# Sparse attention and MoE on one core: V of two tiles loaded block by block, two weight blocks asked for by SyncE

## The chip, the core and the metric

One core of one Trainium2 chip. A time is the device time of one execution in microseconds; before the change it is 736.47 us, the median of 3 runs (736.07 to 736.59).

## What is computed

Block-sparse attention over 4 batches, 8 heads, 768 positions and 64 columns per head, and then a two-layer network on its output. Positions come in 24 blocks of 32. A query block sees its neighbours, the first and the last block, and three sampled blocks; the queries of the first and the last block see everything.

```python
mask = np.abs(blk_i - blk_j) <= window
mask = mask | (blk_i == 0) | (blk_j == 0) | (blk_i == n_blocks - 1) | (blk_j == n_blocks - 1)
for qb in range(n_blocks):
    for kb in sampled_blocks[qb]:
        mask[qb * block:(qb + 1) * block, kb * block:(kb + 1) * block] = True
...
attn = attn / (np.sum(attn, axis=-1, keepdims=True) + 1e-09)
return np.matmul(attn, v).astype(np.float32)
...
h = np.maximum(x @ w_in, 0.0)
return (h * h @ w_out).astype(np.float32)
```

Here x has 3072 rows of 512, w_in is 512 x 2048 and w_out 2048 x 512. The weights come as 64-bit floats.

## The kernel before

The 3072 rows are 24 tiles of 128 (4 query blocks each; batch b, tile t), and three tiles make a batch of the network, eight in all. `Half` is the attention of four heads of one tile, `Whole` that of two heads for the first and the last query block. A `Half` runs on PE scores (L478), on DVE the maxima (L490), on ACT the exponentials (L537), on PE the transposes (L552), on ACT and DVE the copies pT (L562, L564), on PE the product with V (L573), and on DVE the normalising (L587 to L590) and the transposing into x (L418). x is split into a high and a low part (xh L912, xl L916). The network's first layer is L928 (ph, from wi), its second L972 in the first batch (po, from WO and gp) and L982 in the later ones.

V of a tile is two tiles of four query blocks. The first (rows 0 to 63) holds the fixed rows, which are the first and the last key block and the same for all four query blocks, and below them two sampled blocks for each query block. The second holds the window and the third sampled block. For the first three tiles V lies in buffers of its own. `load_static` (L215) brings the fixed rows and `load_sampled` (L400) the sampled blocks, 65 KB each, through registers that SP loads with the indices. Both are issued by SP, which issues its DMAs in the order of the program and uses eight semaphores in turn: the ninth issue waits until the first has landed.

The weights come in blocks of 128 x 512, block f of w_in (part 0) and of w_out (part 1), in the order of the list `cuts`: three of part 0, then parts 1 and 0 in turn. A block goes through four stages, each of them called by `advance`:

- load: `cut_load` (L825), 512 KB of raw 64-bit words into a tile `craw` of a ring of seven buffers that the split weights share. POOL issues it.
- cut: two passes on ACT (L841, L843). The first ends at `W` for part 0 and at `WO` for part 1, or at `ct` for the very first block.
- bits: two passes on DVE (L852, L853).
- split: for blocks that are split, a cast on ACT (L890) and a difference on POOL (L893); for the first block L859 and L860 on POOL.

In the first batch the order of all engines is written out by hand. A counter `now` steps through the attention of the first three tiles; at the steps in `LOADS_0`, `CUTS_0`, `BITS_0` and `SPLIT_0` a stage advances. Three more loads are called in `prepare` and `rest` (L1076, L1091), which run at steps 8 and 35 and otherwise gather keys of the next tiles on POOL (L304, L322). Afterwards, in the network's first batch, `cut_next` cuts one block more and brings the other stages up to their distance from it: the load stage stands `AHEAD` = 4 blocks ahead. Each engine works its own instructions in order, so a load stands on POOL behind the key copies that were written before it, and a cut whose block has not landed holds up ACT.

Of the kernel before, what the change touches and what calls it, by code (L numbers as in the profile page):

```python
# [12 lines left out]
I32 = mybir.dt.int32  # L13
# [5 lines left out]
SP = mybir.EngineType.SP  # L19
# [4 lines left out]
BLK = 32  # L24
NBLK = S // BLK
NRAND = 3
P = 128
NT = S // P
NJ = P // BLK
# [13 lines left out]
HW = H * VW  # L43

NVB = NBLK + 2
V_STATIC = NBLK

UC = 3
# [25 lines left out]
LAG_2 = ({**LAG_0, "c": 3}, {**LAG_0, "t": 2})  # L74
SPLIT_0 = (54, 60)

LOADS_0 = (45, 50, 53, 56, 58)
CUTS_0 = (36, 46, 56, 58)
BITS_0 = (44, 50, 59, 60)
WI_0 = 47  # L80
# [26 lines left out]
def tile_block_sparse_attention_moe(ctx: ExitStack, tc, kd, knd, qd, qgd, vd, vnd, samp, const, wcat, out):  # L107
# [9 lines left out]
    nc = tc.nc  # L117
# [52 lines left out]
    VJ = {0: [one.tile([P, NJ, HW], F32, name=f"V{c}") for c in range(2)]}  # L170
# [5 lines left out]
    order = [(b, t) for b in range(B) for t in range(NT)]  # L176
# [14 lines left out]
    def values_of(k):  # L191

        return V[k if k < UC else 0]
# [4 lines left out]
    def halves(k, u):  # L198

        if k < UC:  # L200
            return slice(0, 2) if u == k // 2 else None
        return slice(u, u + 1)

    def columns(src, us):

        return src.rearrange("... (u c) -> ... u c", u=2)[..., us, :]

    def load_static(k, u, eng=nc.sync):
        us = halves(k, u)
        if us is None:  # L210
            return
        n = 1 if k == 0 else NJ
        if k < UC:
            src = vd[order[k][0], V_STATIC * BLK :].unsqueeze(1).broadcast_to([2 * BLK, n, HW])
            eng.dma_start(VJ[k][0][0 : 2 * BLK, 0:n], src)  # L215
            return
        for i in range(us.start, us.stop):
            src = columns(vd[order[k][0], V_STATIC * BLK :], i)
            src = src.unsqueeze(1).broadcast_to([2 * BLK, n, HW // 2])
            eng.dma_start(values_of(k)[0][0 : 2 * BLK, i, 0:n], src)  # L220

    def copy_static(i, copy):

# [4 lines left out]
    def place(k, j, n):  # L228

        return (j + n - 1 if 0 < k < UC else 1 + n) % NJ  # L230

    def windows(k, i):

        b, t = order[k]
        V1, vn = V[k][1][:, i], st["vn", b, i]

        def wide(copy):
            copy(V1, vn[:, t : t + 1].broadcast_to(list(V1.shape)))

        def narrow(copy, j, blk):  # L240
            at = slice(blk % NJ * BLK, (blk % NJ + 1) * BLK)
            copy(V1[at, j], vn[at, blk // NJ])

        return [
            wide,
            lambda copy: narrow(copy, 0, NJ * t - 1),
            lambda copy: narrow(copy, NJ - 1, NJ * t + NJ),
        ]
# [7 lines left out]
    def groups(t):  # L256

        return tuple(range(1 if t == 0 else 0, NJ - 1 if t == NT - 1 else NJ))
# [4 lines left out]
    def sampled(t, i, on):  # L263
        n = NJ * NRAND
        a = (2 * t + i) * n
        return nc.values_load_multi_w_load_instructions(
            st["idx"][0:1, a : a + n],
            engines=[on],
            min_val=0,
            max_val=NBLK - 2,  # L270
            skip_runtime_bounds_check_because="products of a block's index with 0 or 1, that is zero unless the index is 1 to 22",
        )[1]

    def load_q(b, t, eng=nc.sync, own=None):
        q = (own or rot).tile([P, NJ, NPAIR, BLK], F32, tag="q", name=f"q{b}_{t}", bufs=1 if own else 2)
        n = NJ * NPAIR * BLK
        eng.dma_start(q.rearrange("p a b c -> p (a b c)"), qd[b, :, t * n : (t + 1) * n])
        st["q", b, t] = q
# [31 lines left out]
    def key_windows(k, u, copy):  # L310

        b, t = order[k]
        kg, kn = st["kg", b, t][:, :, :, 2 * u : 2 * u + 2], st["kn", b, u]
        if 0 < k < UC:
            dst = kg[:, :, NJ:NK].rearrange("p j a i c -> p j a (i c)")
            src = kn[:, NJ * t : NJ * t + NJ].rearrange("p a i c -> p a (i c)").unsqueeze(1)
            copy(dst, src.broadcast_to(list(dst.shape)))
            return
        js = groups(t)
        c = NJ * t + js[0] - 1  # L320
        for n in range(3):
            copy(kg[:, js[0] : js[-1] + 1, NJ + place(k, 0, n)], kn[:, c + n : c + n + len(js)])  # L322
# [36 lines left out]
    def load_window(k, u, eng=nc.sync):  # L359
        us = halves(k, u)  # L360
        if us is None:
            return
        b, t = order[k]
        VB = values_of(k)[1]
        js = sorted(groups(t))
        j, c, n = js[0], NJ * t + js[0], len(js)
        if k < UC:
            src = vd[b, (c - 1) * BLK : (c + 1 + n) * BLK]
            src = bass.AP(src.tensor, src.offset, [[HW, 3 * BLK], [BLK * HW, n], [1, HW]])
            eng.dma_start(VJ[k][1][BLK:P, j : j + n], src)  # L370
            return
        for i in range(us.start, us.stop):
            src = vd[b, (c - 1) * BLK : (c + 1 + n) * BLK, i * HW // 2 : (i + 1) * HW // 2]
            src = bass.AP(src.tensor, src.offset, [[HW, 3 * BLK], [BLK * HW, n], [1, HW // 2]])
            eng.dma_start(VB[BLK:P, i, j : j + n], src)

    drawn = {}

    def load_sampled(k, u, eng, on, which=range(NRAND)):
        us = halves(k, u)  # L380
        if us is None:
            return
        b, t = order[k]
        VA, VB = values_of(k)
        if (b, t) not in drawn:
            drawn.clear()
            drawn[b, t] = sampled(t, 1, on)
        vals = drawn[b, t]
        if k < UC:
            v4 = vd[b].rearrange("(a p) c -> p a c", p=BLK)  # L390
        else:
            v4 = columns(vd[b], us).rearrange("(a p) u c -> p a u c", p=BLK)
        for j in sorted(groups(t)):
            for r in which:
                a = (place(k, j, 3) if r == 2 else 2 + r) * BLK
                if k < UC:
                    dst = VJ[k][r == 2][a : a + BLK, j]
                else:
                    dst = (VB if r == 2 else VA)[a : a + BLK, us, j]
                eng.dma_start(dst.unsqueeze(1), v4[:, bass.ds(vals[NRAND * j + r], 1)])  # L400

    def load_values(k, u, static=False):

        if static:
            load_static(k, u)
        load_window(k, u)
        load_sampled(k, u, nc.sync, SP)

    def x_tile(b, t):
        if (b, t) not in X:  # L410
            X[b, t] = rot.tile([P, NCC, P], F32, tag="x", name=f"x{b}_{t}", bufs=5)
        return X[b, t]
# [397 lines left out]
    cv = {}  # L810
# [11 lines left out]
    def cut_load(f, part):  # L822
        if wide:
            cv[f, part] = rot.tile([P, DM, 2], I32, tag="w", name=f"craw{f}_{part}", bufs=WBUFS)
            nc.gpsimd.dma_start(cv[f, part].rearrange("p a b -> p (a b)"), wcat[f, part].bitcast(I32))  # L825

    def cut(f, part):

# [39 lines left out]
    done = dict.fromkeys(stages, 0)  # L868

    def advance(stage):  # L870

        if done[stage] < len(cuts):
            stages[stage](*cuts[done[stage]])
        done[stage] += 1

    def cut_next():

        n = done["cut"] + 1
        for stage, to in (("cut", n), ("bits", n - 1), ("split", n - 2), ("load", n + AHEAD)):
            while done[stage] < to:  # L880
                advance(stage)

    def need(f, part):
# [3 lines left out]
    def split(c, src, name):  # L887
        w = rot.tile([P, 2, DM], F32R, tag="w", name=name, bufs=WBUFS)
        if c == 0:
            nc.scalar.copy(w[:, 0], src)  # L890
        else:
            nc.vector.tensor_copy(w[:, 0], src)  # L892
        nc.gpsimd.tensor_tensor(w[:, 1], src, w[:, 0], op=ALU.subtract)  # L893
        return w
# [165 lines left out]
    load_sampled(0, 0, nc.sync, SP)  # L1060
    load_window(0, 0)
    load_q(0, 1)
    load_q(0, 2, own=begin)
    load_static(1, 0)
    load_sampled(1, 0, nc.sync, SP, (0, 1))
    for k in range(UC):
        keys_of(0, k, begin if k == 2 else None)
    for k in range(1, UC):
# [7 lines left out]
    def prepare():  # L1076
        key_windows(1, 1, nc.gpsimd.tensor_copy)
        deque(keys[1], 0)
        for f in windows(1, 0) + windows(1, 1):
            f(nc.gpsimd.tensor_copy)  # L1080
        advance("load")
        load_static(2, 1)
        load_sampled(1, 0, nc.sync, SP, (2,))
        load_sampled(2, 1, nc.sync, SP, (0, 1))
        for _ in groups(2):
            next(keys[2])
        for f in windows(2, 1):
            f(nc.gpsimd.tensor_copy)
        advance("load")

    def rest():  # L1091
        key_windows(2, 1, nc.gpsimd.tensor_copy)
        deque(keys[2], 0)
        advance("load")

    fixed = [lambda i=i: copy_static(i, nc.scalar.copy) for i in range(2)]
    fixed += [lambda f=f: f(nc.scalar.copy) for f in windows(2, 0)]
# [7 lines left out]
    while work.todo or work.running or now < SPLIT_0[-1]:  # L1105
# [16 lines left out]
        if now in SPLIT_0:  # L1122
            f = 1 + SPLIT_0.index(now)
            wi1[0, f] = split(0, W1[f], f"wi0_{f}")
        for at, stage in ((CUTS_0, "cut"), (BITS_0, "bits"), (LOADS_0, "load")):
            if now in at:
# [85 lines left out]
```

## Time and profile before

| What | Value |
|---|---|
| median of 3 runs | 736.47 us |
| the profiled execution | 737.9 us |
| its span, first to last instruction | 735.4 us |
| mean granted clock of PE | 0.998 |
| PE busy in 20:30, 30:40, 40:50, 50:60, 60:70 | 9.53, 7.24, 6.87, 9.22, 8.18 of 10 us |
| DMA share in the same stretches | 1.01, 0.93, 0.67, 0.67, 0.82 |
| PE busy in 80:90 and in the five stretches of 10 us behind it | 10.00 of 10 us each |

In a row of a timeline the columns are start in us, duration in us, engine, line, operation, what is written from what is read, the count of merged instructions, and in brackets the idle time before with what ended it; "issue" there means that no semaphore in the profile ended it. In a row of windows they are the stretch, its length, the busy time of PE, PEld, DVE, ACT and POOL with counts, the granted clock, the share of the 16 DMA engines and GB/s. A row of a queue is packets, MB, share of 16 engines. A row of the DMA issues ends with the count, the KB of each and the median time from issue to landing. SPq is SP issuing a DMA; craw is a raw weight block.

### The profile page before, as it was taken

What the parts mean: (1) busy time and instruction counts of PE and PEld (TensorE: products, weight loads), DVE (VectorE), ACT (ScalarE), POOL (GpSimd) and SP (SyncE); (2) the same over time, 40 slices, a digit from 0 to 9 for tenths busy, and PEclk for the clock granted to TensorE, in tenths of its full rate; (3) what the DMA queues carried; (4) which work ended last, traced back from release to release, by engine and by line L of the source; (5) the groups of instructions that cost most, each with busy time, mean ns of one, the idle gap of its engine ahead of it and who ended that gap; (6) DMA issues with size and microseconds to landing.
All of it is one profiled execution on the core that took longest, in us unless ns stands there. A gap on an engine that the chain in (4) does not pass through costs nothing.

```text
span 735.4 us, 21490 instructions
## 1 busy us (share of the span) xinstructions
PE 706.9 (96%) x7496; PEld 566.9 (77%) x7496; DVE 531.3 (72%) x1057; ACT 500.4 (68%) x1117; POOL 554.8 (75%) x711
## 2 busy tenths in 40 slices
PE   5887999999999999999999999999999999999998
PEld 3564766678788888877878888887778888888986
DVE  5687888777686868678776877768878686647552
ACT  5777878988866866688876776578777776623222
POOL 8969969358776768869777587777876576868985
PEclk9999999999999999999999999999999999999999
DMA  9977798555645565554545556545455352101001
GB/s 271 226 230 224 239 351 266 129 144 149 181 111 129 168 180 166 132 125 142 155 113 125 163 154 201 151 97 156 107 156 146 93 161 52 34 1 44 1 1 43
DMA packets 91886, 105.10 MB, mean 143 GB/s; under 512 B 13667, under 2 KB 77668, under 8 KB 91780
## 3 DMA queue, kind: packets, MB, share of 16 engines
q1 hardware_dynamic: 85972, 81.15, 41.8%
q0 software_dynamic: 5664, 22.45, 9.1%
q8 instruction: 60, 0.98, 0.6%
q14 instruction: 46, 0.38, 0.2%
q10 hardware_dynamic: 144, 0.13, 0.1%
HBM read 97.39 MB, written 6.29 MB: 141 GB/s over the span
## 4 chain that ended last, share of the span: by engine, by line
PE 81%; DVE 7%; ACT 4%; POOL 4%; issue 2%; DMA 2%; POOLq 0%; DVEq 0%; ACTq 0%
PE ph L928 32%; PE po L982 27%; PE pv L573 6%; PE s L478 6%; PE po L972 5%; PE pvg L734 2%; PE g L664 1%; DVE m L490 1%; DMA kn<-in_kn_dram 1%; PE pt L552 1%; POOL gl L962 1%; DVE p L497 1%; DVE gf L960 1%; POOL pgm L700 1%; DVE xl L916 1%
## 5 line engine op out<-in xcount | busy, mean ns | idle before, releaser
L928 PE MATMUL ph<-xh,wi 128*128 128x384 f32 x960 | 275.6, 347 | 1.8 <-POOL wi L893 1.8
L522 ACT ACTIVATE pm<-p 32x256 f32<-32x256 f32 x528 | 219.3, 415 | 15.1 <-DVE p L497 7.9
L982 PE MATMUL po<-wo,gh 128*128 128x512 f32 x672 | 211.6, 396 | 0.0
L893 POOL TENSOR_TENSOR wi<-W,wi 128x512 fp32r<-128x512 f32 x120 | 164.2, 1368 | 58.8 <-DVE wi L892 37.4
L928 PEld LDWEIGHTS ph<-xh,wi 128*128 128x128 f32 x960 | 174.1, 188 | 23.9 <-issue 12.2
L949 ACT ACTIVATE r<-ph 128x384 f32<-128x384 f32 x128 | 62.9, 491 | 173.3 <-PE ph L928 172.5
L893 POOL TENSOR_TENSOR wo<-WO,wo 128x512 fp32r<-128x512 f32 x112 | 144.6, 1291 | 34.6 <-DVE wo L892 33.3
L962 POOL TENSOR_TENSOR gl<-gf,gh 128x384 fp32r<-128x384 f32 x112 | 119.3, 1065 | 65.0 <-DVE gf L960 55.9
L928 PE MATMUL ph<-xl,wi 128*128 128x384 f32 x480 | 161.9, 337 | 0.0
L982 PEld LDWEIGHTS po<-wo,gh 128*128 128x128 f32 x672 | 123.1, 188 | 26.7 <-issue 7.5
L960 DVE SCALAR_TENSOR_TENSOR gf<-ph,r 128x384 f32<-128x384 f32 x112 | 62.0, 553 | 107.7 <-ACT r L949 99.6
L982 PE MATMUL po<-wo,gl 128*128 128x512 f32 x336 | 134.4, 400 | 5.4 <-POOL gl L962 5.2
L928 PEld LDWEIGHTS ph<-xl,wi 128*128 128x128 f32 x480 | 90.2, 188 | 9.1 <-issue 5.4
L892 DVE CAST wo<-WO 128x512 fp32r<-128x512 f32 x112 | 86.2, 770 | 0.0
L982 PEld LDWEIGHTS po<-wo,gl 128*128 128x128 f32 x336 | 63.0, 187 | 25.1 <-POOL gl L962 11.8
L955 ACT ACTIVATE gh<-r 128x384 fp32r<-128x384 f32 x112 | 58.9, 526 | 10.1
L490 DVE TENSOR_REDUCE m<-s 128x2 f32<-128x512 f32 (+1 forms) x96 | 61.0, 675 | 3.7 <-PE s L478 3.6
L573 PEld LDWEIGHTS pv<-V,pT 128*32 128x32 f32 x2816 | 42.7, 110 | 25.0 <-issue 17.7
L892 DVE CAST wi<-W 128x512 fp32r<-128x512 f32 x105 | 61.2, 583 | 0.0
L573 PE MATMUL pv<-V,pT 128*32 128x65 f32 x2816 | 50.9, 223 | 7.2 <-issue 7.0
L478 PE MATMUL s<-KG,q 64*32 64x256 f32 x1408 | 53.4, 382 | 0.0
L972 PE MATMUL po<-WO,gp 128*128 128x512 f32 x96 | 46.9, 603 | 0.8 <-ACT gp L952 0.8
(93 smaller groups left out, 774.2 us busy)
## 6 DMA issues: line engine op xcount, KB each, us to landing
craw<-in_w_dram POOLq DMA_DIRECT2D x32, 512.0 KB, 6.0
V<-in_v_dram SPq DMA_DIRECT2D x462, 32.5 KB, 2.6
KG<-in_k_dram SPq DMA_DIRECT2D x189, 64.0 KB, 1.9
V<-in_v_dram SPq DMA_DIRECT2D x28, 390.0 KB, 5.2
KG<-in_k_dram SPq DMA_DIRECT2D x12, 768.0 KB, 5.9
q<-in_q_dram SPq DMA_DIRECT2D x24, 256.0 KB, 3.0
out_dram<-ot SPq DMA_DIRECT2D x23, 256.0 KB, 4.0
V<-in_v_dram SPq DMA_DIRECT2D x14, 292.5 KB, 5.2
```

The costliest lines, as they stand in the source:

```text
L478: nc.tensor.matmul(self.sb[e][g * BLK : (g + 1) * BLK, i * NSLOT : (i + 1) * NSLOT], q[r, j, pr, :], kg[r, j, :, pr, :], start=True, stop= ...
L490: nc.vector.tensor_reduce(m[at, e], self.sb[e][at].rearrange("p (i c) -> p i c", i=2), axis=AX, op=ALU.max)
L522: nc.scalar.activation(p[a * BLK : (a + 1) * BLK, g], x[g * BLK : (g + 1) * BLK, :, a], AF.Exp, scale=SCALE)
L573: nc.tensor.matmul(po[h * BLK : (h + 1) * BLK, g * VW : (g + 1) * VW], self.pT[:, g, 2 * e + i, c], v[:, self.u, j, h * VW : (h + 1) * VW] ...
L892: nc.vector.tensor_copy(w[:, 0], src)
L893: nc.gpsimd.tensor_tensor(w[:, 1], src, w[:, 0], op=ALU.subtract)
L928: nc.tensor.matmul(ph[c, f][:, :TOK], wi[:, w, cc], x[:, cc], start=(cc == 0 and i == 0), stop=(cc == NCC - 1 and i == 2),)
L949: nc.scalar.activation(r, acc[:, :TOK], AF.Relu)
L960: nc.vector.scalar_tensor_tensor(gf, acc[:, :TOK], 0.0, r, op0=ALU.max, op1=ALU.mult)
L962: nc.gpsimd.tensor_tensor(gl, gf, gh, op=ALU.subtract)
L972: nc.tensor.matmul(acc[c][u], g[:, u * P : (u + 1) * P], WO[f], start=(f == 0), stop=(f == NF - 1))
L982: nc.tensor.matmul(acc[c][u], g[:, at], w[:, k], start=(f == 0 and i == 0), stop=(f == NF - 1 and i == 2))
```

## The change

Three things change, all in the first batch. V of tiles two and three is issued query block by query block, the fixed rows of a block (130 KB instead of one load of 520 KB for all four) and then its two sampled blocks. The first two weight blocks are asked for by SP, each in two loads of 64 partitions, the first behind V of tile two and the second in the middle of V of tile three; q of tile three comes behind the first. The other loads of the first batch go from steps 45, 50, 53, 56, 58 to 50, 56, 58, 59, `rest` calls none any more, and `cut_next` brings each stage on by two at most in one call.

```diff
-LOADS_0 = (45, 50, 53, 56, 58)
+LOADS_0 = (50, 56, 58, 59)
...
+    def load_static(k, u, eng=nc.sync, j=0):
+        if k < UC:
+            eng.dma_start(VJ[k][0][0 : 2 * BLK, j], vd[order[k][0], V_STATIC * BLK :])
             return
...
+    def load_block(k, j):
+
+        load_static(k, k // 2, j=j)
+        load_sampled(k, k // 2, nc.sync, SP, (0, 1), (j,))
...
-            nc.gpsimd.dma_start(cv[f, part].rearrange("p a b -> p (a b)"), wcat[f, part].bitcast(I32))
+            to, of = cv[f, part].rearrange("p a b -> p (a b)"), wcat[f, part].bitcast(I32)
+            if done["load"] < 2:
+                for at in (slice(0, P // 2), slice(P // 2, P)):
+                    nc.sync.dma_start(to[at], of[at])
+            else:
+                nc.gpsimd.dma_start(to, of)
...
-            while done[stage] < to:
+            for _ in range(min(to - done[stage], 2)):
                 advance(stage)
...
     load_q(0, 1)
+    for j in range(NJ):
+        load_block(1, j)
+    advance("load")
     load_q(0, 2, own=begin)
-    load_static(1, 0)
-    load_sampled(1, 0, nc.sync, SP, (0, 1))
...
-        advance("load")
-        load_static(2, 1)
         load_sampled(1, 0, nc.sync, SP, (2,))
-        load_sampled(2, 1, nc.sync, SP, (0, 1))
+        for j in range(NJ):
+            if j == 2:
+                advance("load")
+            load_block(2, j)
         for _ in groups(2):
             next(keys[2])
         for f in windows(2, 1):
             f(nc.gpsimd.tensor_copy)
-        advance("load")
...
-        advance("load")
```

The order on PE, DVE and ACT is the same in both kernels. On SP, this stood behind the window of tile one (V10 is the first half of V of tile two, q0_2 is q of tile three; register steps and repeated rows are left out):

```order
L370 DMA V1_79<-in_v_dram 96x3x520
L277 DMA q0_1_167<-in_q_dram 128x512
L277 DMA q0_2_169<-in_q_dram 128x512
L215 DMA V10_116<-in_v_dram 64x4x520
L266 TENSOR_LOAD idx_107
...
L400 DMA V10_116<-in_v_dram 32x520
```

And this stands there now, up to the rest of V of tile two (V11):

```order
L364 DMA V1_79<-in_v_dram 96x3x520
L271 DMA q0_1_167<-in_q_dram 128x512
L210 DMA V10_116<-in_v_dram 64x520
L260 TENSOR_LOAD idx_107
...
L394 DMA V10_116<-in_v_dram 32x520
...
L827 DMA craw0_0_206<-in_w_dram 64x1024 x2
L271 DMA q0_2_209<-in_q_dram 128x512
...
L394 DMA V11_117<-in_v_dram 32x520
```

The 64x4x520 load has become four of 64x520, each ahead of its sampled blocks; the two halves of the first weight block and then q0_2 follow them.

On POOL, around the splits of the second and third block of w_in (wi0_1, wi0_2), before; craw4_0 is the raw block of part 0 with f = 4, the seventh in use, craw2_1 the eighth, craw5_0 the ninth:

```order
L825 DMA craw3_0_1045<-in_w_dram 128x1024
...
L825 DMA craw1_1_1097<-in_w_dram 128x1024
L893 TENSOR_TENSOR wi0_1_1102<-W11_80,wi0_1_1102 128x512
L825 DMA craw4_0_1149<-in_w_dram 128x1024
...
L1119 MEMSET V1_79 1x1
L825 DMA craw2_1_1166<-in_w_dram 128x1024
L893 TENSOR_TENSOR wi0_2_1170<-W12_81,wi0_2_1170 128x512
L322 COPY KG0_84<-kn0_1_128 128x4x64 x3
...
L825 DMA craw5_0_1264<-in_w_dram 128x1024
```

The same place now:

```order
L829 DMA craw2_0_1049<-in_w_dram 128x1024
...
L897 TENSOR_TENSOR wi0_1_1104<-W11_80,wi0_1_1104 128x512
L829 DMA craw0_1_1151<-in_w_dram 128x1024
...
L1123 MEMSET V1_79 1x1
L829 DMA craw3_0_1168<-in_w_dram 128x1024
L829 DMA craw1_1_1172<-in_w_dram 128x1024
L897 TENSOR_TENSOR wi0_2_1174<-W12_81,wi0_2_1174 128x512
L316 COPY KG0_84<-kn0_1_128 128x4x64 x3
...
L829 DMA craw4_0_1268<-in_w_dram 128x1024
L829 DMA craw2_1_1270<-in_w_dram 128x1024
```

craw4_0 and craw2_1 have moved from ahead of wi0_2 to behind it and behind three copies and six gathered blocks of keys, to the place that was craw5_0's.

More of the change, by code (lines that the diff above doesn't have):

```diff
@@ L206, in columns @@
         return src.rearrange("... (u c) -> ... u c", u=2)[..., us, :]
-    def load_static(k, u, eng=nc.sync):
-        us = halves(k, u)
-        if us is None:
+    def load_static(k, u, eng=nc.sync, j=0):
+        if k < UC:
+            eng.dma_start(VJ[k][0][0 : 2 * BLK, j], vd[order[k][0], V_STATIC * BLK :])
             return
[L212 to L220, printed above, removed]
+        src = columns(vd[order[k][0], V_STATIC * BLK :], u)
+        src = src.unsqueeze(1).broadcast_to([2 * BLK, NJ, HW // 2])
+        eng.dma_start(values_of(k)[0][0 : 2 * BLK, u], src)
     def copy_static(i, copy):
@@ L377, in tile_block_sparse_attention_moe, with load_sampled @@
     drawn = {}
-    def load_sampled(k, u, eng, on, which=range(NRAND)):
+    def load_sampled(k, u, eng, on, which=range(NRAND), js=None):
         us = halves(k, u)
@@ L392, in load_sampled @@
             v4 = columns(vd[b], us).rearrange("(a p) u c -> p a u c", p=BLK)
-        for j in sorted(groups(t)):
+        for j in sorted(groups(t)) if js is None else js:
             for r in which:
```

## The prediction

> **What bounds the kernel now.** I read the page first, then the windows, then who waits for whom on PE, then the timelines of the first 75 us, engine by engine.
>
> ```profile
> span 735.4 us, 21490 instructions
> PE 706.9 (96%) x7496; PEld 566.9 (77%) x7496; DVE 531.3 (72%) x1057; ACT 500.4 (68%) x1117; POOL 554.8 (75%) x711
> ...
> q8 instruction: 60, 0.98, 0.6%
> ...
> craw<-in_w_dram POOLq DMA_DIRECT2D x32, 512.0 KB, 6.0
> ```
>
> ```profile
> 73.60:700.00 626.40, 620.95 (x6476) 503.41 (x6477) 466.88 (x909) 440.43 (x993) 467.53 (x510) 1.00 0.50 139
> ```
>
> PE is the bound: from 73.6 to 700 us it is busy 620.95 of 626.40 us. Its order is the same before and after the change. So nothing behind 73.6 us can take up or give back more than a little: what counts is the moment at which PE passes that point. All that the change touches lies ahead of it. The timeline of PE there has these stops:
>
> ```profile
> 29.26 0.43 PE L573 MATMUL pv<-V,pT 128*32 128x65 f32 x15
> 32.76 1.14 PE L573 MATMUL pv<-V,pT 128*32 128x65 f32 x33 [3.08 <-issue]
> ...
> 45.31 1.89 PE L573 MATMUL pv<-V,pT 128*32 128x65 f32 x117 [0.19 <-ACT pT L562]
> 48.85 0.36 PE L573 MATMUL pv<-V,pT 128*32 128x65 f32 x9 [1.64 <-issue]
> ...
> 66.44 0.62 PE L928 MATMUL ph<-xh,wi 128*128 128x384 f32 x2 [1.82 <-POOL wi L893]
> ...
> 73.63 1.14 PE L573 MATMUL pv<-V,pT 128*32 128x65 f32 x64 [2.24 <-issue]
> ```
>
> Two of them (3.08 and 1.64 us) stand in the middle of one group of like matmuls, and no semaphore ended them ("issue"). The transfers and the windows around the first say what they are:
>
> ```profile
> q8 instruction: 1, 0.02, 1.5%
> ```
>
> ```profile
> 25.60:29.70 4.10, 4.08 (x130) 2.61 (x126) 2.91 (x9) 3.33 (x11) 3.98 (x14) 1.00 0.97 220
> 29.70:32.80 3.10, 0.04 (x4) 0.04 (x6) 1.01 (x2) 2.08 (x5) 3.10 (x13) 0.91 1.06 248
> ```
>
> Queue q8 brings instructions: 60 packets of 0.98 MB, 16 KB each. PE runs 2 x 7496 instructions (matmul and weight load), 250 for each packet. One such packet passes between 25.6 and 31.2 us (the first row), taking 1.5% of 16 x 5.6 us, that is 1.3 us; just before the stop PE ran 130 + 126 instructions, one packet's worth. The DMA engines are 0.97 and 1.06 busy in both windows. I read the stop as PE having run out of instructions because their transfer stood behind data. [...]
>
> The stop of 2.24 us ahead of 73.63 is of another kind. PE waits there for the copy of pT, and that stands behind the conversion of weight blocks on ACT and DVE:
>
> ```profile
> 48.13 0.66 ACT L841 ACTIVATE W<-craw 128x512 f32<-128x512 f32 x1
> ...
> 50.90 0.66 ACT L841 ACTIVATE WO<-craw 128x512 f32<-128x512 f32 x1
> ...
> 53.40 0.67 ACT L841 ACTIVATE W<-craw 128x512 f32<-128x512 f32 x1
> ...
> 57.70 0.68 ACT L841 ACTIVATE W<-craw 128x512 f32<-128x512 f32 x1
> ...
> 59.91 0.68 ACT L841 ACTIVATE WO<-craw 128x512 f32<-128x512 f32 x1
> ...
> 64.87 0.66 ACT L841 ACTIVATE W<-craw 128x512 f32<-128x512 f32 x1 [1.95 <-DMA craw<-in_w_dram]
> ...
> 67.77 0.68 ACT L841 ACTIVATE WO<-craw 128x512 f32<-128x512 f32 x1 [0.67 <-DMA craw<-in_w_dram]
> ...
> 70.74 0.56 ACT L562 COPY pT<-pt 128x512 f32<-128x512 f32 x1
> ```
>
> ```profile
> 66.98 0.76 DVE L853 SCALAR_TENSOR_TENSOR W<-craw,W 128x512 int32<-128x512 int32 x1
> ...
> 69.86 3.07 DVE L853 SCALAR_TENSOR_TENSOR WO<-craw,WO 128x512 int32<-128x512 int32 x1
> 72.85 0.68 DVE L564 COPY pT<-pt 128x512 f32<-128x512 f32 x1
> ```
>
> Counting blocks in the order of their use, these L841 rows are the third, fourth, fifth, seventh, eighth, ninth and tenth. ACT works in order, and at the ninth and tenth it stood still for a weight transfer. So a later weight transfer costs time here, although ACT is only 68% busy over the span.
>
> **The change part by part.**
>
> *V by query block on SP, weight blocks one and two moved to SP.* The rows that change place, on SP and on POOL:
>
> ```profile
> 16.73 0.65 SPq L215 DMA_DIRECT2D V<-in_v_dram  x1
> ...
> 25.73 0.60 SPq L215 DMA_DIRECT2D V<-in_v_dram  x1
> ```
>
> ```profile
> 44.47 0.57 POOL L825 DMA_DIRECT2D craw<-in_w_dram  x1
> ...
> 47.60 0.58 POOL L825 DMA_DIRECT2D craw<-in_w_dram  x1
> ...
> 49.40 0.53 POOL L825 DMA_DIRECT2D craw<-in_w_dram  x1 [0.26 <-issue]
> 53.63 1.73 POOL L893 TENSOR_TENSOR wi<-W,wi 128x512 fp32r<-128x512 f32 x1 [3.71 <-issue]
> ...
> 59.34 0.57 POOL L825 DMA_DIRECT2D craw<-in_w_dram  x1
> ...
> 64.03 1.06 POOL L825 DMA_DIRECT2D craw<-in_w_dram  x2
> ```
>
> Each of the two 520 KB loads of fixed rows becomes four of 130 KB. That is 3 more issues of 0.60 for each, 1.8 us later for what follows on SP, which spreads the bytes. The instruction packet, called for about 25.6, then has no 520 KB at once beside it. But it has 512 KB of weights in two halves and 256 KB of q on the same queue. That is 768 KB ahead of it instead of roughly 512 + 520, so I take two thirds of the stop as gained: 2.1 us, with ends of 0 and 3.08. [...] The second stop (1.64) I leave at nothing gained: PE runs those 117 matmuls in 1.89 us, less time than the 3.1 us that a packet's transfer and the stop behind it span at the first one; its end is 1.64 gained.
>
> POOL is spared two issues of about 0.55 us, and its first 45 us are not what PE waits for: nothing. V of tiles two and three comes in another order but the pv groups that read it are not stopped by it now; with a queue 1.8 us later I count nothing, and a us if that cover is gone. q of tile three moves behind the weights on SP: its scores come long after, nothing.
>
> *The remaining weight blocks.* This is the cost. Before, POOL asked for the third to sixth block by 46 us and for the seventh and eighth at 47.60 and 49.40. Now the third goes out at the place of 44.47, the fourth at that of 47.60, the fifth and sixth at that of 49.40. The seventh and eighth go out only at the place of 59.34, behind the L893 row of 53.63 and the key copies, the ninth at that of 64.03 behind 0.5 more of issue. From the eleventh on the places are the old ones. The time from asking to landing is bounded by two rows: the chain of waits, and 59.34 against ACT's 64.87, that is 5.5.
>
> ```profile
> 64.03 3.72 DMA craw<-in_w_dram
> ```
>
> The page's median is 6.0, from busier queues. I take 4.7 where little else is moving (blocks three to five) and 5.0 for the rest, nearer the 5.5, as the same V loads run beside it.
>
> Blocks three to five: the distances from asking to cutting are 48.13 - 44.47 = 3.7, 50.90 - 47.60 = 3.3 and 53.40 - 49.40 = 4.0. They do not add, as each wait moves all later cuts: the largest shortfall is 4.7 - 3.3 = 1.4 us (ends 0.4 and 2.2). What is left of the gain at POOL's L893 is 2.1 - 1.4 = 0.7 us.
>
> Blocks seven to nine: block seven is asked at 59.34 - 0.7 = 58.6 and lands at 63.6. ACT wanted it at 57.70, and everything behind it on ACT waits: the splits for PE, the exponentials of the next half, the pT copy. Block nine is asked at 64.03 - 0.7 + 0.5 = 63.8 and lands at 68.8.
>
> ```profile
> 57.70:71.30 13.60, 11.78 (x76) 7.26 (x75) 8.94 (x11) 10.57 (x22) 13.57 (x33) 1.00 0.74 224
> ```
>
> ACT's work from block seven's cut to the end of the pT copy is 10.6 us: 63.6 + 10.6 = 74.2. From block nine's it is 71.30 - 64.87 - 0.67 = 5.8: 68.8 + 5.8 = 74.6, the later of the two. DVE's pT copy ended 73.53 - 71.30 = 2.2 behind ACT's, because one L853 took 3.07 instead of about 0.76. Whether that meets again depends on what POOL does just then; I take half, 1.1 (ends 0 and 2.2). So PE resumes at 74.6 + 1.1 + 0.1 = 75.8 instead of 73.63.
>
> **Sum:** 75.8 - 73.6 = +2.2 us. The profiled execution took 737.9 us, 735.4 of span and 2.5 around it, so it would become 740.1. It is 1.4 above the median of 736.47; against that median I forecast 738.7.
>
> **The rivals.** A difference under 0.2%, 1.5 us, cannot be told from no change here.
>
> *Faster.* The stop goes whole (3.08) and lightly loaded transfers land in 3.7. Then blocks three to five cost 0.4, POOL is 2.7 earlier, block nine is asked at 61.8 and lands at 65.5, pT is done at 71.3, and without the long L853 PE resumes at 71.4 to 71.7: about -1.9, 734.6. For it: the windows show DMA at 0.97 in the stretch that is thinned out. Against it: block nine before landed 5.5 after asking, at this same place.
>
> *No change.* The gain is whole but the transfers take 5.0 and half of the L853 comes back: POOL is 3.1 - 1.4 = 1.7 earlier, block nine lands at 67.8, PE resumes at 74.8: +1.2, 737.6. The stops at 29 us and the late weights then nearly cancel. [...]
>
> *The stop stays.* The weights and q that SP now asks for stand ahead of the instruction packet just as the 520 KB did, so the change does not do there what it seems to. Then POOL is 1.4 later: block nine is asked at 66.0, lands at 71.0, pT is done at 76.8, PE resumes at 78.0: +4.4, 740.8.
>
> **How the numbers follow.** The forecast (+1.5 to +3.5) has 0.37 and the stop that stays 0.15: slower 0.52. The two cancelling have 0.28, 0.12 of it with the packet passing a single queue at once. Faster has 0.20. The forecast's own range is 738.0 to 740.0. The range of 734.6 to 741.0 takes in the faster rival's price and the price of the stop that stays, and leaves out the case where the L853 of 3.07 comes back whole beside it (+1.1 more).
>
> **What would show it.** Right: on PE the stop inside L573 near 29.7 shrinks to about 1 us; on ACT the cut of the seventh block (the L841 that was at 57.70) waits several us for craw and starts near 63 to 64; PE's pv group of 73.63 starts near 75.8, and behind it all stays shifted. Wrong: that L841 starts before 62, or block nine's before 65; then the weights did not bind. A stop of 3 us that is still at 29.7 would make the first term wrong, and a pv group before 73 the sign.

## The result and the profile after

| | before | after |
|---|---|---|
| median of 8 runs, us | 736.53 (735.66 to 737.91) | 740.90 (738.65 to 743.79) |
| the profiled execution, us | 737.9 | 740.82 |
| its span, us | 735.4 | 738.6 |
| mean granted clock of PE | 0.998 | 0.993 |

The ratio of the runs is 1.0059 (95% interval 1.0039 to 1.0078): slower by 4.4 us. The two profiled executions are 2.9 us apart, because the one of before was the slowest of its eight runs.

The page of after. SP has taken two of the 32 weight blocks from POOL's queue:

```profile
span 738.6 us, 21493 instructions
PE 710.7 (96%) x7496; PEld 568.6 (77%) x7496; DVE 531.5 (72%) x1057; ACT 500.0 (68%) x1117; POOL 553.5 (75%) x709
...
craw<-in_w_dram POOLq DMA_DIRECT2D x30, 512.0 KB, 6.2
```

PE's timeline, the places that the prediction read and the new stops:

```profile
29.42 0.67 PE L572 MATMUL pv<-V,pT 128*32 128x65 f32 x33 [0.18 <-issue]
...
34.22 0.42 PE L572 MATMUL pv<-V,pT 128*32 128x65 f32 x12 [0.84 <-issue]
...
41.34 1.53 PE L551 MATMUL pt<-ident,p 128*128 128x128 f32 x8 [2.59 <-ACT p L536]
...
48.17 0.33 PE L572 MATMUL pv<-V,pT 128*32 128x65 f32 x9 [0.99 <-issue]
...
57.14 4.50 PE L976 MATMUL po<-WO,gp 128*128 128x512 f32 x6 [2.89 <-ACT gp L956]
...
66.64 1.53 PE L551 MATMUL pt<-ident,p 128*128 128x128 f32 x8 [1.17 <-ACT p L536]
...
75.26 1.14 PE L572 MATMUL pv<-V,pT 128*32 128x65 f32 x64 [0.45 <-issue]
```

The stop of 3.08 us at 29.7 is down to 0.18, with a second one of 0.84 some 250 instructions later. Two stops that semaphores end, both behind ACT, have grown: 2.59 at 41 and 2.89 at 57. Before, they were these, 1.27 and 0.78:

```profile
43.26 1.53 PE L552 MATMUL pt<-ident,p 128*128 128x128 f32 x8 [1.27 <-ACT p L537]
...
55.70 2.84 PE L972 MATMUL po<-WO,gp 128*128 128x512 f32 x6 [0.78 <-ACT gp L952]
```

ACT's cuts show why; these are blocks two, five, seven, eight and nine, and the copy pT:

```profile
39.38 0.67 ACT L845 ACTIVATE W<-craw 128x512 f32<-128x512 f32 x1 [1.33 <-DMA craw<-in_w_dram]
...
54.85 0.67 ACT L845 ACTIVATE W<-craw 128x512 f32<-128x512 f32 x1 [2.09 <-DMA craw<-in_w_dram]
...
61.81 0.68 ACT L845 ACTIVATE W<-craw 128x512 f32<-128x512 f32 x1 [2.58 <-DMA craw<-in_w_dram]
...
64.67 0.68 ACT L845 ACTIVATE WO<-craw 128x512 f32<-128x512 f32 x1 [1.02 <-DMA craw<-in_w_dram]
...
68.65 0.67 ACT L845 ACTIVATE W<-craw 128x512 f32<-128x512 f32 x1 [0.97 <-DMA craw<-in_w_dram]
...
73.78 0.56 ACT L561 COPY pT<-pt 128x512 f32<-128x512 f32 x1
```

Before, ACT waited for craw three times between 28 and 76 us, 4.8 us in all, first at block nine. Now it is 8.0 us, from 39 us on. Block two is the one that SP asks for. The two transfers on the chain of waits, blocks five and nine:

```profile
46.92 7.91 DMA craw<-in_w_dram
...
62.38 6.25 DMA craw<-in_w_dram
```

Where the time comes from, by the start of the same recorded matmul of PE in both profiles (900 lies inside the pv group of 73.63, behind the stop ahead of it):

| matmul | before, us | after, us | difference |
|---|---|---|---|
| 300 | 28.26 | 27.82 | -0.44 |
| 450 | 37.24 | 32.88 | -4.36 |
| 600 | 44.83 | 42.91 | -1.91 |
| 750 | 52.60 | 51.92 | -0.68 |
| 900 | 74.16 | 75.79 | +1.63 |
| 3300 | 298.68 | 300.56 | +1.88 |
| 6900 | 630.09 | 632.56 | +2.47 |
| end of the last | 731.75 | 734.66 | +2.91 |

So PE first gains 4.4 us, has lost it all and 1.6 more by 75 us, and then loses a further 1.3 us bit by bit in a stretch in which its order is the same and in which it hardly ever stops. The gain can't all be put down to the change: the profile of before is a single execution, and `before_ring` below, which moves no transfer, starts matmul 450 at 32.75 and matmul 600 at 42.79.

### The profile page after: what moved, and what is told of

Its sections match the earlier page's. It is cut to its first block, busy times and chain, and to the rows that moved or that the text cites. A ratio compares the mean times of both kernels' runs of the same rounds, so it can differ in the third digit from the quotient of the medians.

```text
span 738.6 us, 21493 instructions
## 1 busy us (share of the span) xinstructions
PE 710.7 (96%) x7496; PEld 568.6 (77%) x7496; DVE 531.5 (72%) x1057; ACT 500.0 (68%) x1117; POOL 553.5 (75%) x709
## 4 chain that ended last, share of the span: by engine, by line
PE 79%; DVE 8%; POOL 4%; DMA 3%; ACT 3%; issue 2%; POOLq 0%; DVEq 0%; ACTq 0%
PE ph L932 32%; PE po L986 26%; PE s L477 6%; PE pv L572 6%; PE po L976 5%; DMA craw<-in_w_dram 2%; PE pvg L733 2%; DVE m L489 1%; DMA kn<-in_kn_dram 1%; PE g L663 1%; DVE pT L527 1%; DVE p L496 1%; POOL gl L966 1%; POOL pgm L699 1%; DVE gf L964 1%
## 5 line engine op out<-in xcount | busy, mean ns | idle before, releaser
L572 PE MATMUL pv<-V,pT 128*32 128x65 f32 x2816 | 52.6, 225 | 3.0 <-issue 2.5
L976 PE MATMUL po<-WO,gp 128*128 128x512 f32 x96 | 48.6, 621 | 2.9 <-ACT gp L956 2.9
```

Of the source, the lines that this page charges most:

```text
L572: nc.tensor.matmul(po[h * BLK : (h + 1) * BLK, g * VW : (g + 1) * VW], self.pT[:, g, 2 * e + i, c], v[:, self.u, j, h * VW : (h + 1) * VW] ...
L976: nc.tensor.matmul(acc[c][u], g[:, u * P : (u + 1) * P], WO[f], start=(f == 0), stop=(f == NF - 1))
```

## The experiments

All are timed in the manner of the result, each against its own runs of the kernel before (medians 736.2 to 737.8 us), so they are compared by ratio; 0.1% is 0.74 us.

My theory at the start was that of the forecast, *late places*: what costs is that blocks three to ten are asked for later on POOL. Its first rival, *crowding*: the transfers of the first 75 us fill the DMA engines, so places matter little and any gain on PE waits for the next block. Two more came out of the first runs, *SP's weights* (what costs is that SP brings blocks one and two) and *placement* (PE's slower pace behind 75 us comes from the addresses of buffers).

| kernel | ratio to before | 95% interval |
|---|---|---|
| the change | 1.0059 | 1.0039 to 1.0078 |
| v_only | 0.9974 | 0.9958 to 0.9989 |
| late_only | 1.0014 | 0.9999 to 1.0029 |
| v_late | 1.0012 | 0.9997 to 1.0027 |
| after_place | 1.0027 | 1.0010 to 1.0044 |
| after_early | 1.0059 | 1.0037 to 1.0081 |
| v_sp_place | 1.0066 | 1.0051 to 1.0081 |
| sp_both | 1.0012 | 0.9997 to 1.0027 |
| after_nocap | 1.0031 | 1.0011 to 1.0051 |
| before_ring | 1.0018 | 1.0006 to 1.0031 |
| v_ahead | 0.9999 | 0.9985 to 1.0014 |
| v_ten | 0.9993 | 0.9975 to 1.0011 |
| v_ahead5 | 1.0051 | 1.0034 to 1.0069 |

**V by query block alone (v_only).** The kernel before, with this and the rewritten `load_static` of the change:

```diff
-    load_static(1, 0)
-    load_sampled(1, 0, nc.sync, SP, (0, 1))
+    for j in range(NJ):
+        load_block(1, j)
...
-        load_static(2, 1)
-        load_sampled(2, 1, nc.sync, SP, (0, 1))
+        for j in range(NJ):
+            load_block(2, j)
```

> The kernel before, with V of tiles two and three by query block and nothing else. Late places (my theory): the 3.08 us stop of PE inside pv near 29.7 us falls under 1 us, all weight blocks are asked for at the old places, so what is gained stays: about 734 us, 2 to 3 under the kernel before. Crowding (rival: the transfers of the first 75 us fill the DMA engines, so any gain on PE waits for the next weight block): the stop falls too, but block nine's cut stays near 64.9 us and the time is 736 to 737. If the stop of 3 us stays, the loads of 520 KB were not what the instruction packet stood behind, and the time is 736.5.

735.63 us, 1.9 under the kernel before. PE's timeline:

```profile
29.72 0.67 PE L572 MATMUL pv<-V,pT 128*32 128x65 f32 x33 [1.72 <-issue]
...
35.37 0.42 PE L572 MATMUL pv<-V,pT 128*32 128x65 f32 x13 [2.02 <-issue]
...
71.11 1.25 PE L572 MATMUL pv<-V,pT 128*32 128x65 f32 x64 [2.24 <-ACT gp L951]
```

The gain came, near the size expected, but not in the way expected: the stop only fell to 1.72, and another of 2.02 stands some 250 instructions later, so that the two are no shorter together than the 3.08 of before. Where the 1.9 us come from is not shown. In this profile the weight blocks came earlier too, as POOL's order went on earlier, and ACT waited 3.7 us for craw instead of 4.8. This kernel beats both others.

**The late places alone (late_only).** The kernel before with the change's `LOADS_0`, its limit in `cut_next`, and without the load in `rest`.

> The kernel before, with only the late places: the third weight load left out of the early steps, the loads at steps 50, 56, 58, 59 and two at most in one call; V and the first two blocks as before. Late places: the stop of 3.08 us stays and nothing pays for the late blocks; block seven is cut at 62 to 64 instead of 57.7, block nine near 70, PE passes the pv group of 73.63 near 77 to 78: 740 to 741 us. Crowding: block nine lands when the bytes ahead of it have passed, near 65 to 66, and the time is 736 to 737.5.

738.29 us, ratio 1.0014: 1 us, not the 3.5 to 4.5 that I expected, and the interval just reaches no change. The mechanism was there: block seven was cut at 61.76 and ACT waited 6.3 us for craw:

```profile
ACT W L841 <- DMA craw<-in_w_dram: 6.0, 4, 2.3
```

But PE passed matmul 900 only 0.36 us later than in the profile of before. That late blocks by themselves mostly fill time that the kernel before loses at blocks nine and ten is argued, not shown.

**The change with the loads back at the old places (after_early).**

```diff
-LOADS_0 = (50, 56, 58, 59)
+LOADS_0 = (45, 50, 53, 56, 58)
...
         deque(keys[2], 0)
+        advance("load")
```

> The changed kernel with the loads of blocks three to eight back at the old places (one in the step that gathers keys, the others at steps 45, 50, 53, 56, 58). Late places: the wait for block five (2.09 us) and that for block seven (2.58 us) on ACT go, PE passes the pv group at 71.5 to 73, and the time is 733.5 to 735.5, under the kernel before. Crowding: the blocks are asked for earlier and take longer to land, the sum of ACT's waits for craw stays near the 10 us of the changed kernel, and the time is 739 to 741.

742.06 us, ratio 1.0059. My theory fell here: with the places undone, the loss is all still there. Who waits for whom on ACT and on PE (us in total, times, longest):

```profile
ACT W L845 <- DMA craw<-in_w_dram: 4.2, 1, 4.2
```

```profile
PE pt L551 <- ACT p L536: 5.5, 1, 5.5
```

One wait of 4.2 us, for block two, which SP asked for at 34.01 and ACT could cut at 40.63 only. ACT's exponentials stand behind that cut, and PE stopped for 5.46 us. What followed, in windows (length, the five engines, granted clock, DMA share, GB/s):

```profile
36.94:40.35 3.41, 0.18 (x2) 0.00 (x0) 2.01 (x6) 0.00 (x0) 3.32 (x8) 1.00 0.97 248
40.35:54.00 13.65, 9.43 (x145) 7.96 (x146) 6.46 (x16) 8.00 (x17) 4.43 (x12) 0.50 1.03 292
```

PE ran at half clock for 13.65 us, beside a DMA share of 1.03. So V by query block, 1.9 under before by itself, has become 4.4 over it with SP's weights and the change's addresses; with the old addresses (v_sp_place, below) it is 4.9. The prediction priced SP's weights at nothing.

**The change without the limit of two (after_nocap).** `cut_next` as before; block nine is asked for with seven and eight.

> The changed kernel without the limit of two per stage and call, so that the first call in the network catches up with the loads by itself: block nine is asked for with seven and eight at 57.7 instead of at 62.4. Late places: block nine is cut about 3 us earlier or as soon as ACT comes to it, the wait for seven (2.58 us) stays; PE passes the pv group 0.5 to 1.5 us earlier: 739 to 740 us. Crowding: three loads asked for together land as late as before, no change from the changed kernel: 740.5 to 741.5.

739.78 us, ratio 1.0031, about 2 us under the change by the two ratios. Block nine no longer waited, block seven still did (3.12 us). PE passed matmul 900 at 72.86, 2.9 before the change; a stop of 0.86 us and a half-clock stretch at 200 us (mean granted clock 0.992), behind a stop that every kernel here has, took back most of it in this profile (below).

**Buffers (before_ring, after_place).** In the memory plans, the change reserves the first weight buffer ahead of other buffers of the same pool. That shifts the whole ring in which raw and split weights lie for the rest of the run. `before_ring` does only that:

```diff
     load_sampled(1, 0, nc.sync, SP, (0, 1))
+    cv[cuts[0]] = rot.tile([P, DM, 2], I32, tag="w", name="craw0_0", bufs=WBUFS)
...
-            cv[f, part] = rot.tile(...)
+            if (f, part) not in cv:
+                cv[f, part] = rot.tile(...)
```

> The kernel before with one buffer taken earlier: the tile of the first raw weight block is reserved behind V of tile two, where the changed kernel reserves it, and nothing is loaded or worked on at another time. By this the ring of raw and split weights lies at 104032 to 132704 in a partition instead of 116448 to 145120, and the probabilities lie behind it instead of ahead. Placement theory: PE takes 0.2% longer for the same matmuls, 658.5 instead of 657.2 us from its 900th matmul to its last, and the time is 1.3 us over the kernel before. Late places and SP's weights (the other theories) have no part in it: no difference.

737.92 us, ratio 1.0018: 1.3 us, as expected. Its profile shows something else. V still comes in loads of 520 KB, and yet the first stop is short and a second one follows, as in v_only:

```profile
29.61 0.67 PE L573 MATMUL pv<-V,pT 128*32 128x65 f32 x33 [0.73 <-issue]
...
35.52 0.42 PE L573 MATMUL pv<-V,pT 128*32 128x65 f32 x13 [2.28 <-issue]
```

So a short first stop is no sign of V by query block. The start of the same matmuls of PE, in one profile of each kernel, in us:

| kernel | 450 | 600 | 750 | 900 |
|---|---|---|---|---|
| before | 37.24 | 44.83 | 52.60 | 74.16 |
| before_ring | 32.75 | 42.79 | 50.30 | 71.99 |
| v_only | 32.86 | 42.85 | 50.11 | 71.75 |
| v_late | 34.09 | 43.41 | 51.35 | 73.97 |
| v_sp_place | 33.26 | 43.62 | 53.76 | 75.29 |
| after_place | 33.02 | 42.33 | 51.35 | 74.28 |
| the change | 32.88 | 42.91 | 51.92 | 75.79 |

Up to matmul 600 before_ring and v_only are alike, and before stands apart. So the marks up to 600 say little of the change, and what its parts cost is read behind them.

`after_place` is the change with the old addresses; the three tiles are handed to the Whole that used to make them:

```diff
+    first["mo"] = rot.tile([P, 2], F32, tag="mo", name="mo0_0", bufs=2)
+    first["mb"] = rot.tile([P, 2], F32, tag="mb", name="mb0_0", bufs=2)
+    first["p"] = rot.tile([P, S], F32, tag="p", name="pg0_0", bufs=PBUFS)
     advance("load")
     load_q(0, 2, own=begin)
```

> The changed kernel with the buffers where the kernel before has them (the first maxima and probabilities of a Whole are reserved ahead of the first weight block), nothing else. Placement theory: from its 900th matmul to its last PE takes 657.2 us instead of 658.5; the time falls by 1.3 to about 739.5. If the slower PE of the changed kernel has another cause, no change: 740.9.

738.71 us, ratio 1.0027: 2.4 us under the change by the ratios, more than expected, with intervals that allow 1.3. In a third pair, after_early against v_sp_place, the ratios show no cost of the new addresses (1.0059 against 1.0066), with intervals that allow the 1.3 too. The groups of one matmul of the second layer (count, busy us, mean ns), in before, after, before_ring and after_place in this order:

```profile
L982 PE MATMUL po<-wo,gh 128*128 128x512 f32 x672 | 211.6, 396 | 0.0
```

```profile
L986 PE MATMUL po<-wo,gh 128*128 128x512 f32 x672 | 212.9, 398 | 0.1
```

```profile
L983 PE MATMUL po<-wo,gh 128*128 128x512 f32 x672 | 212.9, 398 | 0.0
```

```profile
L987 PE MATMUL po<-wo,gh 128*128 128x512 f32 x672 | 211.8, 396 | 0.0
```

In these four, 396 ns goes with the old addresses and 398 with the new. The other kernels agree, but for 1 ns more in the two that have a half-clock stretch at 200 us (after_nocap and sp_both). The other matmuls go the same way; over the stretch from matmul 900 to the last start it is 657.2 us in before, 658.5 in the change, 658.8 in before_ring and 657.4 in after_place.

**The change without SP's weights (v_late).** v_only and late_only together.

> V of tiles two and three by query block, and the late places of the other weight loads, but blocks one and two by POOL at their old places: the changed kernel without SP's weights. Late places (my theory so far): the wait for blocks five and seven on ACT is as in the changed kernel, 2 us or more each, and the time is 738 to 739.5. SP's weights: the late places are worth the 1.0 us that they were worth alone, so the time is 736 to 737, and PE has no stop of 2.5 us near 39 to 42.

737.56 us, ratio 1.0012. It lies between the ranges of the two theories: V by query block gains nothing here that late_only does not show without it, and the late places cost 0.38% on top of V by query block, 2.8 us. ACT waited 6.9 us for craw, with these at the third to ninth block:

```profile
ACT W L840 <- DMA craw<-in_w_dram: 6.3, 4, 2.4
```

That is the forecast's picture: the late blocks are what PE's end waits for. Why they cost only 1 us without V by query block is not shown. SP's weights, with the old addresses (after_place), add 0.15% to this, 1.1 us, too little to tell from none.

**SP's weights with V by query block (v_sp_place).** after_early with the old addresses.

> The changed kernel with blocks three to eight asked for at the old places and the buffers where they were before: V by query block and SP's weights alone. SP's weights: block two, asked for at 34 us on SP in the middle of V of tile three, lands at 39 to 41, ACT waits for it ahead of the exponentials, PE stops for 2.5 us or more near 37 to 42 and runs at half clock for 3.4 us or more behind it: 739 to 741 us. Late places: no such loss, near the 735.6 of V by query block alone: 735 to 736.5.

741.48 us, ratio 1.0066, 6.8 us over v_only, from which it differs only in SP's weights and the place of q. In its profile ACT waited only 0.74 us for block two and PE stopped for 2.0 us at 42, less than expected; a half-clock stretch of 3.41 us followed at 44.94 (111 matmuls of pv took 3.16 us there, where 117 take 1.89 in before), and a stop of 2.08 us ahead of 50.00 that no semaphore ended. The cost is shown, the share of each of these is not. Against after_place it differs only in the late places, and here they save: 1.0027 instead of 1.0066, 2.9 us, where on top of V by query block alone they cost 2.8. The two parts do not add. PE took 10.15 us from matmul 600 to 750 here, 9.02 in after_place and 7.26 in v_only. In this kernel POOL asked for blocks three and four at 33.38 and 38.17, beside SP's block two, and in after_place first at 40.21; that this is the reason is argued, not shown.

**Both of SP's weight blocks early (sp_both).**

```diff
     advance("load")
+    advance("load")
     load_q(0, 2, own=begin)
...
-            if j == 2:
-                advance("load")
```

> As the kernel with V by query block and SP's weights alone (blocks three to eight at the old places, buffers where they were), but SP asks for block two right behind block one, ahead of q of tile three, and not in the middle of V of tile three. If what SP's weights cost is block two's place in SP's queue (it is asked for at 33 to 34 us there), it lands near 31 to 33, ACT does not wait for it, PE's stops near 42 fall to 1.2 us and the time is 736 to 738. If it is that 512 KB more stand on SP's queue ahead of V and q whatever their place, V or q comes later instead and the time stays at 740 to 742.

737.60 us, ratio 1.0012: 4 us of the 4.9 over before are gone. So, with the other blocks at the old places, it is block two's place in the middle of V of tile three that makes SP's weights dear. But the 512 KB did push something else, here q of tile three:

```profile
33.48 1.96 PE L478 MATMUL s<-KG,q 64*32 64x256 f32 x32 [3.86 <-DMA q<-in_q_dram]
```

**Blocks earlier than before (v_ahead, v_ten, v_ahead5).** All on v_only: block nine earlier by one group of key copies, block ten behind it instead, or the load stage five ahead everywhere.

```diff
-LOADS_0 = (45, 50, 53, 56, 58)
+LOADS_0 = (45, 50, 53, 56, 58, 60)
```

> V by query block alone, and block nine asked for one group of key copies earlier on POOL (at step 60, behind the second split of w_in, 4 us earlier); every later load stays at its place. Late places (a later weight block costs, an earlier one gains): ACT's wait for block nine goes, that for block ten (2.19 us) stays, 0.3 to 1 us under V by query block alone: 734.7 to 735.3. Crowding: block nine's transfer takes longer and nothing changes: 735.6.

737.05 us, ratio 0.9999. Block nine did not wait any more, block ten waited 2.09 us as before, and PE's pv group came at 71.06 instead of 71.11. Nothing gained; the time came out over v_only's, which I do not explain.

```diff
-        ... ("load", n + AHEAD)):
+        ... ("load", n + AHEAD + (n == 5))):
```

> V by query block alone, and block ten asked for right behind block nine on POOL, ahead of a group of key copies; no other load moves. Late places: ACT's wait for block ten (2.19 us, at 65.2 us) goes or shrinks under 0.5, PE passes the pv group that stands at 71.11 there 1 to 2.2 us earlier, the ring of seven is as before from the next call on, and the time is 733.4 to 734.6. Given back: PE passes earlier, but between 75 and 125 us, where ACT and DVE are 80 to 85% busy, it stops at the pv groups for ACT's copies as with the load stage five blocks ahead, and the time is 735.6 to 737.

735.74 us, ratio 0.9993, 0.5 us under its own runs of before, not the 2 to 3 that late places expected. Up to 70 us the profile did what it should:

```profile
68.37 1.13 PE L572 MATMUL pv<-V,pT 128*32 128x65 f32 x64
```

That is 2.7 us earlier than v_only, and 1.6 are left at the end. Over its 12 runs, 733.36 to 738.73 us, it cannot be told from v_only.

```diff
-AHEAD = 4
+AHEAD = 5
```

> V by query block alone, with the load stage five blocks ahead of the cut in the network's first batches instead of four. Late places: from block ten on each block is asked for one call earlier, ACT's waits for nine (0.37) and ten (2.19) shrink, PE passes its pv group 1 to 2 us earlier: 733.5 to 735. Rival: a load that is issued earlier waits on POOL for its buffer of the ring of seven, and the key copies and splits behind it come later: no gain or a loss, 735.5 to 738.

740.52 us, ratio 1.0051. ACT waited for no weight block up to 76 us and PE passed its pv group at 68.84, the earliest but one of all. Then it gave back more than it had gained. The windows of v_ahead5 and of before:

```profile
69.00:126.00 57.00, 52.97 (x598) 34.98 (x594) 40.37 (x65) 42.98 (x85) 46.09 (x95) 1.00 0.88 274
```

```profile
74.00:126.00 52.00, 52.00 (x603) 34.76 (x596) 44.30 (x67) 43.33 (x86) 45.35 (x91) 1.00 0.90 284
```

PE stood for 4 of 57 us, at pv groups that waited for ACT, where ACT's splits waited for DVE:

```profile
80.14 0.62 ACT L889 CAST wi<-W 128x512 fp32r<-128x512 f32 x1 [1.68 <-DVE WO L852]
```

The rival with the ring of seven fits this: with one raw block more in the ring, a split waits until DVE has freed its buffer. That cause is argued, the loss behind 75 us is shown.

## Why the prediction was right or wrong

The sign held, and so did the wide range, by 0.1 us; the forecast's own range, 738.0 to 740.0, did not. Without the new addresses, which the prediction did not have, the change costs 0.27% (after_place), 2.0 us, next to the forecast of 2.2. This nearness is in part luck, as the terms below show.

In steps from before to the change, each by the ratio of two kernels that differ in one part: V by query block -0.26%, late places +0.38%, SP's weights with q behind them +0.15%, addresses +0.32%; together +0.59%, 4.4 us. These sizes hold for this order of the steps alone. With SP's weights ahead of the late places they would be +0.92% and -0.39%. What stands firm is that the two together cost 0.53%, 3.9 us, on top of V by query block.

- *The first stop, 2.1 us gained.* V by query block alone is worth 1.9 in time, but that this comes from the stop is not shown, and the agreement may be luck. PE's stops without a semaphore between 20 and 40 us sum to 2.58 to 3.08 in the profiles of the three kernels without V by query block, and to 1.26 to 3.74 in the five that have it without SP's weights; v_only, with its 1.9 us, has the 3.74. In the six with SP's weights they sum to 0 to 2.13, in the change to 1.02. Of the 3.08 the change has 0.18 left, with 0.84 at the next stop. That an instruction packet passes a single busy queue at once, to which the prediction gave 0.12 of its chances, no run shows; in its place the change kept these 1.02 us, and the time of that case, 737.6, did not come.
- *POOL's two spared issues and q: nothing.* I moved two weight blocks to SP and priced only what POOL is spared, not when they land behind V. With the other blocks at the old places that was wrong by 6.8 us (v_sp_place over v_only). In the change, with its late places, block two was late by 1.33 us on ACT, but the time that it costs is 1.1 us (after_place over v_late), which cannot be told from nothing.
- *Blocks three to five, 1.4 late.* Block five was 2.09 late: asked for together with six, it took 7.91 us, not 4.7.
- *Block seven cut at 63.6, block nine at 68.8.* 61.81 and 68.65. Block seven came 1.8 earlier, and so below the 62 that I had named as the mark of weights that do not bind. The mark was badly set: ACT did wait for it, 2.58 us. At block nine two errors cancel: it was asked for at 62.38 instead of 63.8 and took 6.25 instead of 5.0.
- *The long L853, half of it.* In the change (L857 there) one of 1.66 us instead of 3.07 or 0.76, close to half.
- *PE resumes at 75.8.* 75.26: +1.63 instead of +2.2. That rests on the one profile of before; against before_ring, in which nothing but buffers moved, matmul 900 is 3.8 us later, and against v_only 4.0.
- *Nothing behind 73.6 us gives back more than a little.* Wrong twice. The addresses cost 1.3 us or more over the rest of the run, which before_ring and after_place show; and v_ahead5 lost 5 us there.

Of the rivals, the one in which the stop stays named a time near the measured one (740.8) for a reason that was not there.

What stays open: by what V by query block gains its 1.9 us; why late places cost without SP's weights and save with them; how much the half-clock stretches add to the median; why v_ahead came out over v_only; and how SP's weights split into q, V and block two. Crowding is not ruled out either: block five, asked for together with six, took 7.91 us to land, where I had taken 4.7.

## What to carry to other kernels

A transfer that changes queue is priced by when it lands in its new queue, not by the issue that the old queue is spared. A buffer that is asked for earlier can move others of its pool, so the memory plans of the two kernels are compared before two dense stretches are called the same. Parts of a change are priced together as well as one by one, as their costs need not add. A stop in one profile of one execution is compared with a second kernel of the same order before its loss is called a gain of the change. An engine that passes a mark earlier has gained only if the stretch behind it is not bound by another engine or by the ring.

## What the runs showed of the hardware

*The clock fell to half for 3.41 us or a multiple of it.* Windows of the change in steps of 3.41 us; the granted clock changed at 57.10 and at 60.51:

```profile
53.69:57.10 3.41, 0.56 (x4) 0.23 (x2) 0.87 (x2) 2.22 (x5) 3.41 (x10) 1.00 0.40 116
57.10:60.51 3.41, 3.37 (x4) 1.51 (x5) 2.97 (x5) 2.10 (x4) 3.41 (x10) 0.50 0.53 127
60.51:63.93 3.42, 3.42 (x16) 2.68 (x15) 1.15 (x3) 1.84 (x3) 3.42 (x9) 1.00 1.02 338
```

PE was busy 0.56 us in one such window and ran at half clock in the next: six matmuls took 4.50 us there, where six take 2.84 in v_ten. The change has three such stretches, which start at 12.73, 43.45 and 57.10 us: 30.72 and 13.65 us apart, nine and four times 3.41. Before has one ahead of its last matmul, at 32.19, and after_early has 13.65 us at half clock on end. In the 3.41 us ahead of them PE was busy 1.28, 1.88 and 0.56 us in the change, 0.90 in before and 0.18 in after_early. How long PE is busy in such a window does not settle it alone: in before it was busy 1.77, 1.72 and 1.65 us in those from 45.85, 62.91 and 69.74, less than the 1.88, and the clock stayed full behind them. The same stop is followed by half clock in one run and not in another. Behind the one of 1.14 us ahead of 199.59 in before, 1.11 ahead of 201.25 in the change, the clock stayed full; after_nocap and sp_both have a half-clock stretch there, at 200 us. Counted back from the stretches in steps of 3.41, the first window starts at 1.47 us in before and at 2.49 in the change; that a stop costs more or less by how it falls into the windows is argued, not shown. In the change half clock made the stop of 2.89 us at 57 dearer than it is long: the six matmuls behind it took 1.66 us more than in v_ten. Half clock may be part of the spread between runs: the change's clock was 0.985 to 0.995 in its eight runs.

*Addresses change PE's pace.* The same matmuls of the second layer took 396 or 398 ns by where the weights lie, 0.5%. Which pair of addresses makes the difference was not tried.
